# Attention on one core: every unit's finished row maxima go through DRAM with their parts made on VectorE, prepared weights are stored a task later, reciprocals come a key tile later

## The chip, the cores and the metric

The kernel runs on one core of one Trainium2 chip. The metric is device time in microseconds; a kernel's time is the median of its runs. A profiled execution is one further run, taken by the hardware profiler; its span reaches from its first to its last instruction.

The core's engines have one instruction queue each: TensorE (PE, matmuls into PSUM, with its weight loads as PEld), VectorE (DVE), ScalarE (ACT), GpSimd (POOL) and SyncE (SP), which issues nearly all of this kernel's DMAs.

## The reference

One transformer block for 2048 rows of width 640: attention with 32 heads of 20 columns, then a gated feed-forward layer of width 1728.

```python
def _A_ref(x, wqkv, wo):
    qkv = (x @ wqkv).reshape(B, S, 3, H, Dh)  # then split into q, k, v per head
    scores = jnp.einsum("bhqd,bhkd->bhqk", q, k) * (Dh ** -0.5)
    p = _softmax(scores, axis=-1)
    o = jnp.einsum("bhqk,bhkd->bhqd", p, v)
    return o.transpose(0, 2, 1, 3).reshape(B, S, D) @ wo

def _B_ref(x, w_gate, w_up, w_down):
    return (_silu(x @ w_gate) * (x @ w_up)) @ w_down

h = x + _A_ref(_layernorm(x, axis=-1), A_wqkv, A_wo)
h2 = h + _B_ref(_layernorm(h, axis=-1), B_w_gate, B_w_up, B_w_down)
```

The output is h2. All is float32. The softmax subtracts each row's maximum before the exponential.

## The kernel before, in words

The program has three stages: the projections to q, k and v (to about 317 us), the attention (to about 1437 us), and the output projection with the feed-forward layer.

**Units and key tiles.** The attention stage is a loop over 32 units u. A unit is one group g of 4 heads (u // 4) and one chunk of 512 queries (u % 4). Inside, a loop goes over 16 key tiles kt of 128 keys. A key tile of a unit is a string of steps, ORDER (L41), which alternates between "WsSmmSsM" and "WSsMMsSm". "s" and "S" are the scores of one head (L1303, a TensorE matmul, then an exponential on ScalarE, L1309); "W" is the weighing of the key tile two back (L1313, eight matmuls of the probabilities with the values), followed by what is due at this key tile; "m" and "M" are one step each of the maxima.

**The maxima** of later units are built ahead, three steps in each key tile (`max_one`): one matmul of queries with 512 keys into one of three PSUM banks `ps_max` (L274), and a VectorE reduction of that bank (L280). The list `rest` says which unit's step is next, and with it where a unit v is complete: v = 4g at key tile 5 of unit 4g − 1, v = 4g + 1 at key tile 15 of that unit, v = 4g + 2 at key tile 5 of unit 4g + 1, and v = 4g + 3 at key tile 10 of unit 4g + 2, the unit just ahead of it. The first, v = 1, is complete at key tile 10 of unit 0.

**What happens to complete maxima.** At the end of the key tile `max_all` (L287) reduces the unit's partial maxima and negates them: 128 query rows by 16 numbers (4 heads, 4 query tiles). They are needed as rows along the queries, in two float32r parts each (a rounded part and the rest), under the queries in `q_stk`: the scores' matmul of 62 rows takes the subtraction along, so a unit's first scores wait for them. Before, there are two ways to it.

- Nine units (v = 1, and every v = 4g + 3) go through `max_finish`, two key tiles later: a TensorE transpose (L319), a ScalarE copy as first part (L89), a VectorE subtraction as second part (L90), and four DMAs from SBUF to SBUF (L326).
- The other 22 go through DRAM. `max_parts` makes the two parts at once, on POOL (cast L295, subtract L296); `max_turn`, four key tiles later, transposes blocks of 32 by 32 on VectorE (L303) and stores them to `m_d` (L304); `max_load`, six key tiles after completion, loads the rows by four DMAs (L314). `m_d` has two places, for odd and even units.

Unit 0's own maxima go through `max_finish` inside the projection stage.

**The end of a unit.** A unit's sums of exponentials come out of the accumulator by a copy and four small DMAs (L1326). At key tile 4 of the next unit VectorE takes the reciprocals (L1334), SP stores them (L1336) and loads them spread over the partitions, as `rb` (L1342). At key tile 9 POOL multiplies the output by `rb` (L1348); at key tile 11 SP issues four stores of it to `o_d` (L1351). The last two units use key tiles 3, 6 and 7.

**Weights prepared on the side.** From unit 1 on, at every key tile but 3 and 4, one task of a list is taken at step W (`prepare_weights`): a load of raw weights (L1141, L1195), two empty tasks, sums on POOL (L1153 to L1158, L1211 to L1217), and pieces, each a cast and a subtraction on POOL (L1121, L1122). Each task first issues, on SP, the DMA stores of the pieces that stand in the list `stores` (L1112); a piece's store is thus issued with the task after it. SP's queue also takes the loads of queries, keys and values (L176, L193).

**SP's order.** SP issues its DMAs in program order. An instruction that must wait, for a piece that POOL hasn't finished, or for an earlier DMA, holds up all behind it.

Of the kernel before, what the change touches and what calls it, by code (L numbers as in the profile page):

```python
# [26 lines left out]
NC = S // CH  # L27
# [17 lines left out]
def tile_block(ctx: ExitStack, tc: tile.TileContext, x, wqkv, wo, wg, wu, wd, out):  # L45
    nc = tc.nc
# [41 lines left out]
    def split(src, hi, lo, lo_engine=nc.vector):  # L88
        nc.scalar.activation(hi, src, AF.Copy)  # L89
        lo_engine.tensor_tensor(out=lo, in0=src, in1=hi.bitcast(F32), op=ALU.subtract)  # L90
# [193 lines left out]
    def max_all(u):  # L284

        ends[u] = stk.tile([P, G * TPC], F32, name="neg", tag="neg", bufs=2)
        nc.vector.tensor_reduce(  # L287
            ends[u], mxs[u].rearrange("p b h t k -> p (b h t) k"), axis=AX.X, op=ALU.max, negate=True
        )

    def max_parts(u):

        neg = ends[u]
        both = ends[u] = stk.tile([P, 2, G * TPC], F32R, name="neg2", bufs=2)
        nc.gpsimd.tensor_copy(both[:, 0], neg)  # L295
        nc.gpsimd.tensor_tensor(  # L296
            out=both[:, 1], in0=neg, in1=both[:, 0].bitcast(F32), op=ALU.subtract
        )

    def max_turn(u):  # L300

        turned = stk.tile([P, 2 * G * TPC], F32, name="turned", bufs=2)
        nc.vector.transpose(turned, ends.pop(u).bitcast(F32).rearrange("p i n -> p (i n)"))  # L303
        nc.sync.dma_start(m_d[u % 2], turned)  # L304

    def max_load(u):

        n = 2 * TPC
        rows = m_d[u % 2].rearrange("(q i r) c -> i r q c", q=4, i=2)
        for b in range(2):  # L310
            for i in range(2):
                row = b * ROW + NPART + i
                dst = queries[u][row : row + 1].bitcast(F32).rearrange("r j c -> r (j c)")
                nc.sync.dma_start(dst, rows[i, b * n : (b + 1) * n])  # L314

    def max_finish(u):

        m = (ps_one if u else ps_max)()[: G * TPC, :P]
        nc.tensor.transpose(m, ends.pop(u), ident)  # L319
        parts = stk.tile([G * TPC, 2, P], F32R, name="m2", tag="m2", bufs=1)  # L320
        split(m, parts[:, 0], parts[:, 1], nc.vector)
        for b in range(2):
            for i in range(2):
                row = b * ROW + NPART + i
                first = b * 2 * TPC
                nc.sync.dma_start(  # L326
                    queries[u][row : row + 1].bitcast(F32).rearrange(
                        "r j (t p) -> r (j t) p", t=TPC
                    ),
                    parts[first : first + 2 * TPC, i, :].bitcast(F32),  # L330
                )
# [33 lines left out]
    with tc.tile_pool(name="pa", bufs=2) as pa:  # L365
# [244 lines left out]
        stores = []  # L610

        def store(*last, queue=nc.gpsimd):

            while stores:
                queue.dma_start(*stores.pop(0))
            stores.extend(last)
# [487 lines left out]
    def prepare_weights():  # L1104


        stores, count = [], [0]

        def store():
            while stores:  # L1110
                dst, t = stores.pop(0)
                nc.sync.dma_start(dst.bitcast(F32), t.bitcast(F32))  # L1112

# [123 lines left out]
        tasks = []  # L1237
        for f in range(NF):
            tasks += block(f)
        for f in range(0, NF, 2):  # L1240
            if f < NF - 2:
                tasks += rows((f, f + 1), True)
            if f in d_d:
                tasks += rows((f, f + 1), False)
        return tasks + [store]

    class Ring:

# [49 lines left out]
    def scores(u, kt, j, probs):  # L1298

        p, b = divmod(j, 2)  # L1300
        rows = slice(b * ROW, b * ROW + NPART + 2)
        ps = ps_one()
        nc.tensor.matmul(  # L1303
            ps,
            keys[u // NC][rows, p, kt * P : (kt + 1) * P],
            queries[u][rows, p, :],
            start=True, stop=True,
        )
        nc.scalar.activation(probs[p][:, b, :], ps, AF.Exp, scale=scale)  # L1309
# [45 lines left out]
    todo, tail, accs, later, full, now = [], [], {}, {}, [], [0]  # L1355
    singles = [[(*a, b) for a in rest] for b in range(2)]
    left = {u: sum(2 for a in rest if a[0] == u) for u in range(1, NU)}

    def next_max(b):
        if singles[b]:  # L1360
            a = singles[b].pop(0)
            max_one(*a)
            left[a[0]] -= 1
            if left[a[0]] == 0:
                full.append(a[0])

    def weigh_next():
        u, kt, probs = todo.pop(0)
        if kt == 0:
            accs[u] = psum.tile([P, CH], F32, name="acc", tag=f"ps_{last % 3}")  # L1370
        weigh(u, kt, probs, accs[u])
        if kt == NT - 1:
            queues = [nc.sync] if u + 1 < NU else [nc.scalar, nc.sync]
            tail.append((u, *row_sums(accs.pop(u), *queues)))
# [3 lines left out]
    for u in range(NU):  # L1378
        g, c = divmod(u, NC)
        if g == NG - 1 and c >= 2:  # L1380
            _, first, ln, flips, _ = ahead
            extra = [*first, *ln, lambda: None, *flips]
        for kt in range(NT):
            now[0] = u * NT + kt
            probs = [pp.tile([P, 2, CH], F32, name="probs") for _ in range(2)]
            heads = [[0, 2], [1, 3]]
            order = ORDER[now[0] % 2] if singles[0] or singles[1] else "WsSsS"
            for op in order:
                if op in "mM":
                    next_max(int(op == "M"))  # L1390
                elif op in "sS":
                    scores(u, kt, heads[op == "S"].pop(0), probs)
                else:
                    if len(todo) == 2:
                        weigh_next()
                    for f in later.pop(now[0], ()):
                        f()
                    if extra:
                        extra.pop(0)()
                    if preparing and u and kt not in (3, 4):  # L1400
                        preparing.pop(0)()
                    if now[0] == (NU - NC) * NT + 8:
                        unit_ring, last_ring = weight_rings()
                        unit_ring.fill()
                        last_ring.fill()
            todo.append((u, kt, probs))
            for v in full:
                max_all(v)
                if v % NC == NC - 1 or v == 1:
                    later.setdefault(now[0] + 2, []).append(lambda v=v: max_finish(v))  # L1410
                else:
                    max_parts(v)
                    later.setdefault(now[0] + 4, []).append(lambda v=v: max_turn(v))
                    later.setdefault(now[0] + 6, []).append(lambda v=v: max_load(v))
            full.clear()
            if kt == 6 and u + 3 < NU:
                load_queries(u + 3)
            if kt == 10 and u == 0:
                fill_ones(k_stk[1])
            if kt >= 8 and kt % 2 == 0 and c == 1 and g + 1 < NG:  # L1420
                load_keys(g + 1, slice((kt - 8) // 2 * CH, (kt - 6) // 2 * CH))
            if kt >= 8 and kt % 2 == 0 and c == 2 and g + 1 < NG:
                load_values(g + 1, (kt - 8) // 2 * TPC, (kt - 6) // 2 * TPC)

            sooner = u >= NU - 2
            if kt == (3 if sooner else 4) and tail:
                reciprocals(u - 1, tail[0][2], nc.sync)
                rb = spread(u - 1, nc.sync)
            if kt == (6 if sooner else 9) and tail:
                store_o(u - 1, tail[0][1], rb, nc.gpsimd, None)  # L1430
            if kt == (7 if sooner else 11) and tail:
                store_o(u - 1, tail.pop()[1], rb, None, nc.sync)
            if g == NG - 1 and c >= 1:
                at = 8 if sooner else NT - 4
                if kt == at:
                    ahead = projection(
                        c - 1, ps_max if c < NC - 1 else (lambda: ps_b())
                    )
                if kt in (at, at + 1, 12 if sooner else 14):
                    ahead[0][min(kt - at, 2)]()  # L1440
                    if kt == at + 1 and c < NC - 1:
                        ahead[4]()
            k = 2 * (u - NU + 8)
            if kt in (12, 13) and 0 <= k + kt - 12 < ND:
                if k + kt == 12:
                    assert not preparing
                    wo_hi = pc.tile([P, ND, D], F32R, name="wo_hi", bufs=1)
                    wo_lo = pc.tile([P, ND, D], F32R, name="wo_lo", bufs=1)
                load_wo(k + kt - 12)
            if kt in (2, 3) and 0 <= k + kt - 4 < ND:  # L1450
                split_wo(k + kt - 4)
# [573 lines left out]
```

## Time and profile before

| what | us |
|---|---|
| median of 3 runs | 2018.49 |
| lowest and highest run | 2018.06, 2019.48 |
| the profiled execution | 2017.19 |
| its span | 2015.4 |

The granted TensorE clock of the profiled execution is 1.00. In rows of the profile, a group of instructions is given as line, engine, operation, output<-inputs, sizes and count, then busy time and mean duration of one in ns, then the idle time of the engine just ahead of them, with what ended most of it. A row of a timeline begins with the start and the duration in us; what stands in brackets at its end is the idle time ahead of it and who ended it. Rows of SP ("SPq") are the issues of DMAs, not their transfers. The rows that the argument needs are shown where it uses them.

### The profile page before, as it was taken

How to read it: one execution, taken by the hardware profiler on the slowest of the kernel's cores; microseconds unless marked ns; L12 is line 12 of the kernel's file. 1: busy time of each engine (PE TensorE's matmuls, PEld its weight loads, DVE VectorE, ACT ScalarE, POOL GpSimd, SP SyncE). 2: the span in 40 equal slices, each digit the busy share in tenths (PEclk: the TensorE clock that was granted, in tenths of full speed). 3: DMA queues.
4: the chain of work that ended last, by engine and by line, in shares of the span. 5: the costliest groups of instructions: out<-in, count | busy, mean ns of one | idle time of the engine just before them, and what ended most of it. 6: DMA issues, size and time to landing. Idle time of an engine off the chain costs nothing.

```text
span 2015.4 us, 40030 instructions
## 1 busy us (share of the span) xinstructions
PE 2002.7 (99%) x14354; PEld 1247.8 (62%) x14354; DVE 1603.9 (80%) x2806; ACT 1437.1 (71%) x2819; POOL 796.8 (40%) x1190
## 2 busy tenths in 40 slices
PE   9999999999999999999999999999999999999999
PEld 8999995333333333333333333345598888888888
DVE  5677778888888888888888988886387666676677
ACT  4678878999999999999999999986633222212221
POOL 7465423333443443343400011011156444754555
PEclk9999999999999999999999999999999999999999
DMA  7777563352634544535513022321159654974642
GB/s 252 255 251 264 179 204 86 117 150 92 190 104 135 159 128 133 160 122 164 172 40 88 22 75 71 94 63 56 40 185 312 223 187 154 354 274 156 206 150 94
DMA packets 199340, 310.35 MB, mean 154 GB/s; under 512 B 53744, under 2 KB 87856, under 8 KB 198120
## 3 DMA queue, kind: packets, MB, share of 16 engines
q1 hardware_dynamic: 192552, 284.21, 43.8%
q0 software_dynamic: 6496, 23.60, 3.9%
q8 instruction: 114, 1.87, 0.4%
q14 instruction: 82, 0.67, 0.1%
q10 hardware_dynamic: 96, 0.00, 0.0%
HBM read 208.11 MB, written 99.19 MB: 152 GB/s over the span
## 4 chain that ended last, share of the span: by engine, by line
PE 96%; DMA 1%; DVE 1%; POOL 1%; issue 0%; ACT 0%; SPq 0%; POOLq 0%; DVEq 0%; ACTq 0%
PE acc L1313 24%; PE ps_a L1481 17%; PE ps_one L1303 15%; PE ps_max L274 12%; PE ps_one L643 10%; PE ps_b L1576 9%; PE ps_max L239 3%; PE ps_max L1031 2%; PE ps_b L1031 2%; PE ps_two L805 0%; PE ps_two L696 0%; DVE mx L261 0%; DMA rb<-r_d 0%; DVE mx L280 0%; PE ps_max L1066 0%
## 5 line engine op out<-in xcount | busy, mean ns | idle before, releaser
L1309 ACT ACTIVATE probs<-ps_one 128x512 f32<-128x512 f32 x2048 | 1056.1, 612 | 61.9 <-PE ps_one L1303 35.0
L280 DVE TENSOR_REDUCE mx<-ps_max 128x1 f32<-128x512 f32 x1472 | 924.5, 683 | 107.0 <-PE ps_one L1303 73.2
L1303 PE MATMUL ps_one<-q_stk,k_stk 62*128 62x512 f32 x2048 | 580.6, 449 | 1.0 <-DMA q_stk<-m_d 1.0
L1313 PE MATMUL acc<-probs,v_stk 128*32 128x512 f32 x4096 | 546.3, 605 | 0.1
L1303 PEld LDWEIGHTS ps_one<-q_stk,k_stk 62*128 62x128 f32 x2048 | 248.0, 184 | 436.6 <-ACT probs L1309 413.9
L274 PE MATMUL ps_max<-k_stk,q_stk 60*128 60x512 f32 x1472 | 374.9, 426 | 1.1 <-DVE mx L261 0.9
L274 PEld LDWEIGHTS ps_max<-k_stk,q_stk 60*128 60x128 f32 x1472 | 272.5, 186 | 29.7 <-DVE mx L280 2.8
L1698 DVE TENSOR_TENSOR tmp<-ps_a,tmp 128x512 f32<-128x512 f32 x208 | 141.2, 689 | 121.0 <-PE ps_a L1481 94.0
L261 DVE TENSOR_REDUCE mx<-ps_max 128x2 f32<-128x512 f32 x288 | 180.6, 684 | 63.8 <-PE ps_max L239 60.2
L1313 PEld LDWEIGHTS acc<-probs,v_stk 128*32 128x32 f32 x4096 | 80.9, 108 | 179.8 <-issue 167.9
L251 ACT ACTIVATE ps_max<-ps_max 128x512 f32<-128x512 f32 x288 | 151.6, 583 | 42.8 <-PE ps_max L239 40.2
L1576 PE MATMUL ps_b<-halves,yp 128*128 128x320 f32 x1032 | 178.7, 308 | 0.2 <-DVE h L1581 0.2
L1576 PEld LDWEIGHTS ps_b<-halves,yp 128*128 128x128 f32 x1032 | 165.2, 188 | 16.0 <-DVE h L1581 0.5
L1481 PE MATMUL ps_a<-t,units 128*128 128x512 f32 x624 | 162.5, 396 | 0.0
L90 POOL TENSOR_TENSOR yp<-y,yp 128x256 fp32r<-128x256 f32 x96 | 60.4, 630 | 186.9 <-ACT yp L89 186.9
L1481 PE MATMUL ps_a<-z,units 128*128 128x512 f32 x516 | 133.9, 394 | 0.0
L1481 PEld LDWEIGHTS ps_a<-t,units 128*128 128x128 f32 x624 | 112.6, 188 | 18.5
L1348 POOL TENSOR_TENSOR o<-o,rb 128x512 f32<-128x512 f32 x31 | 39.9, 1286 | 199.8 <-DMA q_stk<-m_d 72.7
L1581 DVE TENSOR_TENSOR h<-ps_b,h 128x320 f32<-128x320 f32 x248 | 109.7, 480 | 5.8 <-PE ps_b L1576 4.3
L643 PE MATMUL ps_one<-z_hi,w_lo 64*128 64x512 f32 x380 | 113.3, 392 | 0.0
L643 PE MATMUL ps_one<-z_lo,w_hi 64*128 64x512 f32 x380 | 112.1, 392 | 0.0
L643 PE MATMUL ps_one<-z_hi,w_hi 64*128 64x512 f32 x380 | 111.5, 393 | 0.0
(224 smaller groups left out, 2651.7 us busy)
## 6 DMA issues: line engine op xcount, KB each, us to landing
units<-w_d SPq DMA_DIRECT2D x186, 256.0 KB
w_d<-stage SPq DMA_DIRECT2D x106, 256.0 KB
halves<-j_d SPq DMA_DIRECT2D x70, 320.0 KB
j_d<-stage SPq DMA_DIRECT2D x42, 320.0 KB
k_stk<-k_d SPq DMA_DIRECT2D x64, 160.0 KB
q_stk<-q_d SPq DMA_DIRECT2D x64, 160.0 KB
raw<-k_d SPq DMA_DIRECT2D x62, 160.0 KB
raw<-q_d SPq DMA_DIRECT2D x54, 160.0 KB
```

Source lines behind the costliest of these rows:

```text
L251: nc.scalar.activation(ps, ps, AF.Relu)
L261: nc.vector.tensor_reduce(mx[:, b, :, t, kc], ps.rearrange("p (j n) -> p j n", j=2), axis=AX.X, op=ALU.max,)
L274: nc.tensor.matmul(ps, queries[u][rows, pair, t * P : (t + 1) * P], keys[u // NC][rows, pair, kc * CH : (kc + 1) * CH], start=True, stop=True,
L280: nc.vector.tensor_reduce(mxs[u][:, b, pair, t, kc : kc + 1], ps, axis=AX.X, op=ALU.max)
L643: nc.tensor.matmul(ps, a[rows], b[rows], start=(i == n == 0), stop=(i == 1 and n == last), skip_group_check=True,)
L1303: nc.tensor.matmul(ps, keys[u // NC][rows, p, kt * P : (kt + 1) * P], queries[u][rows, p, :], start=True, stop=True,)
L1309: nc.scalar.activation(probs[p][:, b, :], ps, AF.Exp, scale=scale)
L1313: nc.tensor.matmul(acc[32 * j : 32 * j + 32, :], values[u // NC][:, kt, j * VW : j * VW + 32], probs[j // 2][:, j % 2, :], start=(kt == 0) ...
L1481: nc.tensor.matmul(ps.rearrange("p (t n) -> p t n", t=TPC), w[k][:, i], z[k][:, :, j], start=(first and m == 0), stop=(last and m == len(n ...
L1576: nc.tensor.matmul(ps, a, b, start=(n == 0), stop=(n == len(pairs) - 1))
L1581: nc.vector.tensor_tensor(out=h, in0=ps, in1=h, op=ALU.add)
L1698: add = lambda out, ps, x: nc.vector.tensor_tensor(out=out, in0=ps, in1=x, op=ALU.add)
```

## The change

`max_parts` puts its cast and its subtraction on VectorE in the place of POOL. All 31 units from v = 1 on take the way through DRAM; the turn comes one key tile after completion (four before), the load three key tiles after (six before, and two for the way through TensorE). `max_finish` remains for unit 0 alone. In `prepare_weights` the list of stores keeps its newest piece for one task more, so each store is issued two tasks after its piece; the last task stores all. The reciprocals, their store and their spread load move from key tile 4 to 5, POOL's multiply from 9 to 10; the stores of the output stay at 11. In the last two units these stay as they were.

```diff
@@ max_parts
-        nc.gpsimd.tensor_copy(both[:, 0], neg)
-        nc.gpsimd.tensor_tensor(
+        nc.vector.tensor_copy(both[:, 0], neg)
+        nc.vector.tensor_tensor(
             out=both[:, 1], in0=neg, in1=both[:, 0].bitcast(F32), op=ALU.subtract
         )
@@ prepare_weights
-        def store():
-            while stores:
+        def store(left=1):
+            while len(stores) > left:
                 dst, t = stores.pop(0)
                 nc.sync.dma_start(dst.bitcast(F32), t.bitcast(F32))
...
-        return tasks + [store]
+        return tasks + [lambda: store(0)]
@@ the loop over key tiles
             for v in full:
                 max_all(v)
-                if v % NC == NC - 1 or v == 1:
-                    later.setdefault(now[0] + 2, []).append(lambda v=v: max_finish(v))
-                else:
-                    max_parts(v)
-                    later.setdefault(now[0] + 4, []).append(lambda v=v: max_turn(v))
-                    later.setdefault(now[0] + 6, []).append(lambda v=v: max_load(v))
+                max_parts(v)
+                later.setdefault(now[0] + 1, []).append(lambda v=v: max_turn(v))
+                later.setdefault(now[0] + 3, []).append(lambda v=v: max_load(v))
...
-            if kt == (3 if sooner else 4) and tail:
+            if kt == (3 if sooner else 5) and tail:
                 reciprocals(u - 1, tail[0][2], nc.sync)
                 rb = spread(u - 1, nc.sync)
-            if kt == (6 if sooner else 9) and tail:
+            if kt == (6 if sooner else 10) and tail:
                 store_o(u - 1, tail[0][1], rb, nc.gpsimd, None)
```

What this moves can be seen in the order of the instructions. First VectorE's queue in unit 3, around key tile 5, where the maxima of unit 4 (`mx_130`) are complete and those of unit 5 (`mx_131`) go on. Before:

```order
L280 TENSOR_REDUCE mx_131<-ps_max 128x1 x2
L287 TENSOR_REDUCE neg<-mx_130 128x16
L280 TENSOR_REDUCE mx_131<-ps_max 128x1 x9
L303 STREAM_TRANSPOSE turned<-neg_7288 128x32
L280 TENSOR_REDUCE mx_131<-ps_max 128x1 x21
```

After:

```order
L280 TENSOR_REDUCE mx_131<-ps_max 128x1 x2
L287 TENSOR_REDUCE neg<-mx_130 128x16
L295 CAST neg_7285<-neg 128x16
L296 TENSOR_TENSOR neg_7285<-neg,neg_7285 128x16
L1334 RECIPROCAL r<-r 128x16
L303 STREAM_TRANSPOSE turned<-neg_7285 128x32
L280 TENSOR_REDUCE mx_131<-ps_max 128x1 x30
```

Three reductions are one key tile. L287 and the transpose stood in two places, three key tiles apart; now five small operations stand between two reductions.

Then SP's queue in unit 14, behind the spread load `rb` and the loads of queries: `j_d` and `d_d` are prepared pieces that are stored, `raw` is a load of weights, `v_stk` one of values, `o_d` the output of unit 13, and `q_stk` takes the maxima of unit 15. Before:

```order
L1112 DMA j_d_96<-stage 128x640
L1195 DMA raw<-in_B_w_down 128x640 x2
L193 DMA v_stk_126<-v_d 128x4x96 x2
L1112 DMA d_d_90<-stage 128x640
L1351 DMA o_d<-o 20x512 x4
L326 DMA q_stk<-m_13092 1x8x128 x4
L1112 DMA d_d_90<-stage 128x640
L193 DMA v_stk_126<-v_d 128x4x96
```

After:

```order
L1112 DMA j_d_96<-stage 128x640
L1195 DMA raw<-in_B_w_down 128x640 x2
L193 DMA v_stk_126<-v_d 128x4x96 x2
L304 DMA m_d_71<-turned 128x32
L1112 DMA j_d_96<-stage 128x640
L1351 DMA o_d<-o 20x512 x4
L1112 DMA d_d_90<-stage 128x640
L193 DMA v_stk_126<-v_d 128x4x96
L314 DMA q_stk<-m_d_71 1x32x32 x4
```

The loads of the maxima have moved behind one more piece and one load of values, and a store of the maxima stands ahead of the output's stores.

Last POOL's queue at the same place, with the multiply of unit 13's output in it. Before:

```order
L1121 CAST stage<-sums 128x320
L1122 TENSOR_TENSOR stage<-sums,stage 128x320
L1348 TENSOR_TENSOR o<-o,rb 128x512
L1121 CAST stage<-raw 128x320
L1122 TENSOR_TENSOR stage<-raw,stage 128x320
```

After:

```order
L1121 CAST stage<-sums 128x320
L1122 TENSOR_TENSOR stage<-sums,stage 128x320
L1121 CAST stage<-raw 128x320
L1122 TENSOR_TENSOR stage<-raw,stage 128x320
L1348 TENSOR_TENSOR o<-o,rb 128x512
```

The multiply stands behind one piece more.

## The prediction

> **What bounds the kernel now.** I read the page first: the span, and the busy share of each engine.
>
> ```profile
> span 2015.4 us, 40030 instructions
> PE 2002.7 (99%) x14354; PEld 1247.8 (62%) x14354; DVE 1603.9 (80%) x2806; ACT 1437.1 (71%) x2819; POOL 796.8 (40%) x1190
> ```
>
> TensorE is busy for 99% of the span, so time is lost or won only where TensorE stands still, or where an instruction of its own comes or goes. The profiled execution took 2017.19 us, 1.8 us more than its span, and lies 1.3 us under the median of the three runs, 2018.49; I make the sum on 2017.2 and put 1.3 on at the end. A difference under 0.2%, about 4 us, is what a measurement of this kernel could not tell from no change.
>
> The change touches the attention stage, so next I read the busy times of 50 us inside it (columns: TensorE, weight loads, VectorE, ScalarE, POOL, granted clock, DMA share, GB/s), then VectorE's timeline in a quiet place.
>
> ```profile
> 850.00:900.00 50.00, 50.00 (x355) 19.48 (x349) 44.98 (x76) 48.82 (x96) 25.15 (x37) 1.00 0.43 150
> 926.12 1.89 DVE L280 TENSOR_REDUCE mx<-ps_max 128x1 f32<-128x512 f32 x3 [0.23 <-PE ps_one L1303]
> 928.23 1.29 DVE L280 TENSOR_REDUCE mx<-ps_max 128x1 f32<-128x512 f32 x2 [0.23 <-PE ps_one L1303]
> ```
>
> TensorE fills all 50 us at a granted clock of 1.00. A key tile lasts 928.23 − 926.12 = 2.11 us. In it VectorE reduces three banks of maxima without a pause (1.89 us) and then waits 0.23 us for TensorE. Those 0.23 us are all the room VectorE has, since its three banks of PSUM are what TensorE fills next: a VectorE that is late by more holds TensorE up. So the bound is TensorE, with VectorE close behind it.
>
> How much lateness reaches TensorE can be read off two places where the trace of before has VectorE late, because a reciprocal had to wait for its sums. For each, VectorE's rows come first, then TensorE's weighing matmuls, which stand once in each key tile. Unit 10:
>
> ```profile
> 670.72 1.89 DVE L280 TENSOR_REDUCE mx<-ps_max 128x1 f32<-128x512 f32 x3 [0.23 <-PE ps_one L1303]
> 673.75 0.25 DVE L1334 RECIPROCAL r<-r 128x16 f32<-128x16 f32 x1 [1.15 <-DMA r<-o]
> 673.92 1.82 DVE L280 TENSOR_REDUCE mx<-ps_max 128x1 f32<-128x512 f32 x3
> ```
>
> ```profile
> 673.19 1.06 PE L1313 MATMUL acc<-probs,v_stk 128*32 128x512 f32 x8
> ```
>
> and a key tile on
>
> ```profile
> 676.22 1.06 PE L1313 MATMUL acc<-probs,v_stk 128*32 128x512 f32 x8
> ```
>
> The next three reductions were due at 670.72 + 2.11 = 672.83 and came at 673.92, 1.09 late; TensorE took 3.03 us instead of 2.11, a loss of 0.92. Unit 18:
>
> ```profile
> 946.43 1.89 DVE L280 TENSOR_REDUCE mx<-ps_max 128x1 f32<-128x512 f32 x3 [0.23 <-PE ps_one L1303]
> ...
> 949.21 1.22 DVE L280 TENSOR_REDUCE mx<-ps_max 128x1 f32<-128x512 f32 x2
> ```
>
> ```profile
> 948.91 1.06 PE L1313 MATMUL acc<-probs,v_stk 128*32 128x512 f32 x8
> ```
>
> and a key tile on
>
> ```profile
> 951.50 1.07 PE L1313 MATMUL acc<-probs,v_stk 128*32 128x512 f32 x8
> ```
>
> They came at 949.21 instead of 948.54, 0.67 late; TensorE took 2.59, a loss of 0.48. So about 0.18 us of lateness is swallowed, and the rest is lost one for one.
>
> **The change part by part.** *The parts on VectorE.* Grouped by line over the attention stage (317 to 1437 us), these are the operations concerned.
>
> ```profile
> L1334 DVE RECIPROCAL r<-r 128x16 f32<-128x16 f32 x31 | 7.5, 243 | 1.9 <-DMA r<-o 1.9
> L287 DVE TENSOR_REDUCE neg<-mx 128x16 f32<-128x64 f32 x31 | 6.6, 214 | 0.6
> L303 DVE STREAM_TRANSPOSE turned<-neg 128x32 f32<-128x32 f32 x22 | 4.4, 200 | 0.0
> ```
>
> And the two on POOL that move:
>
> ```profile
> L296 POOL TENSOR_TENSOR neg<-neg,neg 128x16 fp32r<-128x16 f32 x22 | 4.9, 222 | 1.8
> L295 POOL CAST neg<-neg 128x16 fp32r<-128x16 f32 x22 | 4.3, 197 | 255.4 <-DVE neg L287 255.4
> ```
>
> Before, L287 (0.214) and the transpose (0.200) of a unit stood in two different gaps between threes of reductions, and each fits into 0.23 us. After, the order puts L287, cast, subtract, for 15 of the units the reciprocal too, and the transpose into one gap, since the transpose is now due one key tile later and at the head of it. VectorE's price for a cast and a subtract of 16 elements is not in this trace. The nearest rows are three small operations that depend on each other:
>
> ```profile
> 1503.18 0.17 DVE L99 TENSOR_TENSOR t_late<-t_late,v_late 128x8 f32<-128x8 f32 x1
> 1503.38 0.17 DVE L99 SCALAR_TENSOR_TENSOR r_late<-t_late,r_late 128x8 f32<-128x8 f32 x1
> ```
>
> A dependent operation starts 0.20 us after the one before it; an independent one starts before the other ends (the reciprocal at 673.75 lasts 0.25 and the reduction follows at 673.92, an overlap of 0.08). I take 0.20 each. Without the reciprocal the chain is L287 0.21 + cast 0.20 + subtract 0.20 + transpose 0.20 = 0.81, less an overlap of 0.08 at its end: 0.73 to 0.81. With the reciprocal it is about as long: the reciprocal depends on none of its neighbours, so it overlaps on both sides and adds about 0.08, and L287 there stands two reductions behind the last one that it needs, so it starts 0.08 early. I take 0.77 for both. Less the gap of 0.23 VectorE is 0.54 late, less 0.18 TensorE loses 0.36. Thirty units pay (v = 1 to 30; that of unit 31 falls where VectorE has nothing left to reduce): 30 × 0.36 = **+10.8**. Bounds: 0.17 a unit, 5 in all, if cast and subtract overlap so far that each adds 0.10; 0.5 a unit, 15 in all, if they cost 0.25 each.
>
> [...]
>
> [...] In one place of this trace a tiny VectorE operation beside a long POOL one was stretched to the other's end:
>
> ```profile
> 115.69 1.84 POOL L90 TENSOR_TENSOR z_lo<-z_lo 128x768 fp32r<-128x768 f32 x1 [2.05 <-ACT z_lo L89]
> 115.73 1.83 DVE L99 TENSOR_SCALAR r_a<-v_a 128x4 int32<-128x4 int32 x1
> ```
>
> POOL was busy 25.15 of the 50 us above, with prepared weights, and 20 of the 30 new pairs fall where it prepares them. If one of the two operations met half of a POOL operation of some 0.9 us each time it would be 20 × 0.5 × 0.45 = 4.5; if never, nothing. No small VectorE operation of the attention stage is stretched on average in the rows above, so I take **+2**, with 0 to 6.
>
> [...]
>
> *The transposes through TensorE.* Nine units lose their finish by a TensorE transpose, a ScalarE copy and a VectorE subtract. One of them:
>
> ```profile
> 343.54 1.06 PE L1313 MATMUL acc<-probs,v_stk 128*32 128x512 f32 x8
> 344.53 0.28 PE L319 MATMUL ps_one<-ident,neg 128*16 128x128 f32 x1
> ...
> 345.92 1.06 PE L1313 MATMUL acc<-probs,v_stk 128*32 128x512 f32 x8
> ```
>
> That key tile took 2.38 instead of 2.11: 0.27 × 9 = **−2.4**. ScalarE's nine copies go too, and it does not set the pace.
>
> *Old stalls that go.* The two reciprocals that waited (0.92 and 0.48) come a key tile later, 2.1 us, more than the 1.15 they waited. And unit 18's first scores waited for their maxima, whose load now starts three key tiles earlier, at key tile 8 instead of 11:
>
> ```profile
> 932.86 3.21 SPq L314 DMA_DIRECT2D q_stk<-m_d  x4
> ```
>
> ```profile
> 937.44 0.47 PE L1303 MATMUL ps_one<-q_stk,k_stk 62*128 62x512 f32 x1 [1.01 <-DMA q_stk<-m_d]
> ```
>
> 0.92 + 0.48 + 1.0 = **−2.4**. These rows also give the tail of such a load: issuing ends at 936.07, and TensorE goes on 1.4 us later.
>
> *What is queued on SP.* SP issues in order, and each row below is an issue. The unit looked at is 14, where the maxima of unit 15 are completed at key tile 10. SP's queue first, then POOL, then TensorE's first scores of unit 15.
>
> ```profile
> 812.74 0.59 SPq L1342 DMA_DIRECT2D rb<-r_d  x1
> ```
>
> ```profile
> 819.20 1.08 SPq L1195 DMA_DIRECT2D raw<-in_B_w_down  x2
> ```
>
> ```profile
> 827.46 1.55 SPq L1351 DMA_DIRECT2D o_d<-o  x4
> 829.11 2.82 SPq L326 DMA_DIRECT2D q_stk<-m  x4
> 832.03 0.39 SPq L1112 DMA_DIRECT2D d_d<-stage  x1
> 832.48 0.43 SPq L193 DMA_DIRECT2D v_stk<-v_d  x1
> ```
>
> ```profile
> 819.49 1.28 POOL L1348 TENSOR_TENSOR o<-o,rb 128x512 f32<-128x512 f32 x1 [14.17 <-DMA rb<-r_d]
> 825.64 0.45 POOL L1121 CAST stage<-raw 128x320 fp32r<-128x320 f32 x1 [4.87 <-DMA raw<-in_B_w_down]
> 826.18 0.88 POOL L1122 TENSOR_TENSOR stage<-raw,stage 128x320 fp32r<-128x320 f32 x1
> ```
>
> ```profile
> 833.64 0.51 PE L1303 MATMUL ps_one<-q_stk,k_stk 62*128 62x512 f32 x2
> ```
>
> Issue of rb at 812.74 to its landing, which frees SP for the raw load, was 6.5 us, and the raw load fed POOL 6.4 us after its issue. Here the maxima were ready 1.4 us after 831.93, at 833.3, 0.3 us ahead of the scores that need them. With the reciprocal a key tile later, rb and the raw load come up to 2.1 us later, and POOL's multiply now stands behind the first piece: it starts at 827.0 at the earliest, at 829.1 if the raw load is 2.1 later, and ends between 828.3 and 830.4. Behind it SP issues the stores of o (1.55), now also one prepared piece (0.39) and one load of values (0.43), and only then the four loads of maxima (2.82): issued by 833.5 to 835.6, usable 834.9 to 837.0 against 833.64. TensorE would stand 1.3 to 3.3 us in the place of 0.3 us of slack; I take 1.8, nearer the lower end, because only the first of the four must land for the first scores. The same order stands in units 6, 10 and 18; I take 1.8 for units 10, 14 and 18 and nothing for 6, where there is more slack: **+5**, with 0 to 10.
>
> *At nothing:* POOL losing its casts and 255.4 us in line for VectorE (it is not on the path; if it were late, rb's multiply would be, which is the SP term); the stores a task later, which fill a queue that waits for POOL anyway and would cost one 0.39 us issue if not. *Sum:* 2017.2 + 10.8 + 2 + 5 − 2.4 − 2.4 = 2030.2, and 1.3 to the median: **2031.5 us**.
>
> **The rivals.** *Faster: the chain is hidden.* If cast and subtract run back to back with their neighbours, the gap grows to under 0.41 us and TensorE swallows it, the queue is no later than before, and only the gains are left: 2018.5 − 4.8 = 2013.7. For it: 0.23 + 0.18 us are free, and the old waits are real. Against: L287 and the transpose alone fill 0.41. Chance 0.10. *No change.* The chain at its low end, +5, against the gains of 4.8, and all loads in time: 2018.7. Chance 0.13. *Slower, but SP in time.* 10.8 + 2 − 4.8: 2026.5. It decides whether the four loads land before TensorE comes to the next unit; for it, TensorE itself comes later by what VectorE costs. Chance 0.30. *The forecast*, VectorE and SP both late, 2031.5 and up to 2044 with each term at its upper end: 0.47.
>
> **How the numbers follow.** Slower is the last two, 0.77; same 0.13; faster 0.10. Leaving out the faster case and the upper end of the forecast leaves out about 2 in 10: from 2018.5 (chain at 5, no lateness on SP) to 2040.
>
> **What would show it.** In the profile after: gaps of about 0.77 us between threes of reductions at each unit's completion, with the next weighing 0.36 us late, 30 times; nothing left of a TensorE wait on the transposes; casts and subtracts of L295 and L296 at about 0.2 us, longer beside POOL; and TensorE's first scores of units 11, 15 and 19 waiting for q_stk from m_d by some 1.8 us each. The prediction is wrong if weighing stays at 2.11 us apart across these gaps, or if the waits on m_d are nought.

## The result and the profile after

The changed kernel takes 2038.51 us (median of 5 runs, 2035.59 to 2042.63); the kernel before, measured again with it, 2018.49 (2016.96 to 2020.14). The ratio is 1.0101, with a 95% interval of 1.009 to 1.0112: the change makes the kernel 20 us slower. The profiled execution took 2040.52 us, against 2017.19 for that of before: 23.3 us to be explained in the two traces.

The page's span and busy times of the changed kernel:

```profile
span 2038.7 us, 40000 instructions
PE 2019.2 (99%) x14345; PEld 1251.8 (61%) x14345; DVE 1612.5 (79%) x2868; ACT 1437.9 (71%) x2810; POOL 786.0 (39%) x1146
```

TensorE has nine instructions fewer and is busy 16.5 us longer. VectorE gained only 8.6 us of work. So most of the lost time counts as busy on TensorE, though its work did not grow, and the busy share doesn't tell where a span went. The two traces are therefore compared key tile by key tile, by the distance from one key tile's first exponential (L1309) to the next one's. These exponentials start between 318.3 and 1452.9 us in the trace of before, so the stage ends some 16 us later than the 1437 us given above, and between 320.2 and 1475.1 in the trace of after. Places that differ by more than 0.1 us, in sums (us):

```text
30 key tiles behind the chain on VectorE, where no operation in it was stretched   0.36 to 0.47 each: +12.3
the same places, what stretched operations add                                     +3.2
8 places that had a transpose through TensorE                                       -0.26 each: -2.1
units 10 and 18: reciprocals and first scores that waited before                    -0.92 -0.48 -1.13 = -2.5
starts of units 7, 11, 15, 19                                                       0.78 + 3.15 + 2.83 + 0.44 = +7.2
unit 0, key tiles 1 and 2                                                           +2.9
before the attention stage +1.9, after it +1.1                                      +3.0
```

The sum is 24.0 against 23.3; the small differences that the table leaves out come to −0.7. The last line need not be the change's: over the 13 traces of this study the stage's first exponential starts anywhere from 318.3 to 323.0 us, though no edit touches what is ahead of it, and the trace of before is the earliest. Now the views that carry these lines. First the chain itself: VectorE in unit 3, at the place whose order was shown above.

```profile
441.30 0.21 DVE L287 TENSOR_REDUCE neg<-mx 128x16 f32<-128x64 f32 x1
441.54 0.17 DVE L295 CAST neg<-neg 128x16 fp32r<-128x16 f32 x1
441.75 0.17 DVE L296 TENSOR_TENSOR neg<-neg,neg 128x16 fp32r<-128x16 f32 x1
441.92 0.25 DVE L1334 RECIPROCAL r<-r 128x16 f32<-128x16 f32 x1
442.09 0.15 DVE L303 STREAM_TRANSPOSE turned<-neg 128x32 f32<-128x32 f32 x1
442.17 3.63 DVE L280 TENSOR_REDUCE mx<-ps_max 128x1 f32<-128x512 f32 x6
```

From L287's start to the next reduction are 0.87 us. TensorE's weighing matmuls around it:

```profile
441.96 1.06 PE L1313 MATMUL acc<-probs,v_stk 128*32 128x512 f32 x8
444.49 1.06 PE L1313 MATMUL acc<-probs,v_stk 128*32 128x512 f32 x8
```

They start 2.53 us apart; the one ahead of them (439.84) stands 2.12 before the first. Six reductions then run without a pause, as they did behind the late reciprocals of before. So much for the chain alone. At the start of unit 8 VectorE and POOL stand like this:

```profile
602.07 0.22 DVE L287 TENSOR_REDUCE neg<-mx 128x16 f32<-128x64 f32 x1
602.32 0.68 DVE L295 CAST neg<-neg 128x16 fp32r<-128x16 f32 x1
603.04 0.66 DVE L296 TENSOR_TENSOR neg<-neg,neg 128x16 fp32r<-128x16 f32 x1
```

```profile
601.55 0.73 POOL L1154 TENSOR_TENSOR sums<-sums,raw 128x256 f32<-128x256 f32 x1
602.24 0.73 POOL L1157 TENSOR_TENSOR sums<-raw 128x256 f32<-128x256 f32 x1
602.94 0.73 POOL L1158 TENSOR_TENSOR sums<-raw,sums 128x256 f32<-128x256 f32 x1
```

Cast and subtract take 0.68 and 0.66 instead of 0.17 each; both end about where a POOL operation does (602.97, 603.67). That key tile lost 1.38 us, not 0.38. The means of the groups are 229 and 215 ns, against 175 in most of the 31 places, where nothing disturbs them: (54 + 40) ns × 31 = 2.9 us, near the 3.2 of the key tiles. Five casts and four subtracts carry it (0.30 us and more each).

```profile
L295 DVE CAST neg<-neg 128x16 fp32r<-128x16 f32 x31 | 7.1, 229 | 1.1
L296 DVE TENSOR_TENSOR neg<-neg,neg 128x16 fp32r<-128x16 f32 x31 | 6.7, 215 | 1.1
L287 DVE TENSOR_REDUCE neg<-mx 128x16 f32<-128x64 f32 x31 | 6.7, 215 | 0.6
```

L287, a reduction, kept its time: 0.215 us on average, 0.214 before.

Then TensorE's waits, in the list of waits (total, times, longest):

```profile
PE ps_one L1303 <- DMA q_stk<-m_d: 3.5, 4, 1.5
...
PE ps_one L1303 <- ACT probs L1309: 1.4, 2, 0.8
```

The kernel before had one such wait on `m_d`, 1.0 us. How the longest came about can be followed in unit 14, on SP, on POOL and on TensorE:

```profile
832.18 3.60 SPq L1195 DMA_DIRECT2D raw<-in_B_w_down  x2
...
844.29 1.41 SPq L1351 DMA_DIRECT2D o_d<-o  x4
845.75 0.34 SPq L1112 DMA_DIRECT2D d_d<-stage  x1
846.13 0.43 SPq L193 DMA_DIRECT2D v_stk<-v_d  x1
846.61 2.78 SPq L314 DMA_DIRECT2D q_stk<-m_d  x4
```

```profile
841.62 0.45 POOL L1121 CAST stage<-raw 128x320 fp32r<-128x320 f32 x1 [15.23 <-DMA raw<-in_B_w_down]
842.15 0.87 POOL L1122 TENSOR_TENSOR stage<-raw,stage 128x320 fp32r<-128x320 f32 x1
842.98 1.29 POOL L1348 TENSOR_TENSOR o<-o,rb 128x512 f32<-128x512 f32 x1
```

```profile
849.47 0.47 PE L1303 MATMUL ps_one<-q_stk,k_stk 62*128 62x512 f32 x1 [1.47 <-DMA q_stk<-m_d]
851.05 0.47 PE L1303 MATMUL ps_one<-q_stk,k_stk 62*128 62x512 f32 x1 [1.11 <-DMA q_stk<-m_d]
```

The raw weights arrive at 841.6, POOL makes one piece of them before it may multiply, the output's stores wait for the multiply until 844.29, and the loads of the maxima stand behind those, with two other issues between. TensorE gets them 1.47 and 1.11 us late, first for one pair of heads, then for the other.

Last, what was not in the forecast at all. At the start of unit 11 TensorE waits twice:

```profile
706.77 0.46 PE L1303 MATMUL ps_one<-q_stk,k_stk 62*128 62x512 f32 x1 [0.63 <-DMA q_stk<-m_d]
707.99 0.47 PE L1303 MATMUL ps_one<-q_stk,k_stk 62*128 62x512 f32 x1 [0.76 <-ACT probs L1309]
```

The second wait is put down to ScalarE, but it is the wait for the second half of the maxima that unit 15 shows with its own name: in the trace the last of the four loads lands at 707.85, and TensorE goes on at 707.99. Then the granted clock (the seventh entry, between POOL's busy time and the DMA share) falls:

```profile
705.00:709.00 4.00, 2.61 (x21) 1.00 (x23) 2.07 (x4) 2.65 (x7) 3.76 (x8) 1.00 0.56 169
709.00:713.00 4.00, 4.00 (x23) 1.41 (x21) 2.79 (x6) 3.47 (x8) 1.84 (x4) 0.57 0.60 187
713.00:717.00 4.00, 4.00 (x34) 1.67 (x30) 2.98 (x5) 3.14 (x7) 0.00 (x0) 1.00 0.59 194
```

In the trace's record of the clock it is 0.5 for 3.41 us from 709.32 on, 1.7 us lost behind 1.4 us of waiting; and 0.5 for 6.83 us from 323.62 on, in unit 0, 2.4 us behind the end of a wait of 0.93, which costs the 2.9 us of the table. The wait, and the busy times behind it:

```profile
321.25 0.50 PE L274 MATMUL ps_max<-k_stk,q_stk 60*128 60x512 f32 x1 [0.93 <-DVE mx L261]
```

```profile
325.00:331.00 6.00, 6.00 (x29) 2.18 (x22) 2.27 (x4) 2.29 (x5) 5.00 (x2) 0.55 0.39 129
```

That wait in unit 0 stands in the trace of before too, where the clock kept 1.00. So part of the 20 us is clock: the five runs were granted 0.997, 0.999, 0.996, 0.998 and 0.999, in the order of 2040.52, 2035.59, 2042.63, 2038.51 and 2037.78 us. Each 0.001 is 2.04 us of such a run; put back to a full clock, all five lie by that estimate between 2033.6 and 2035.7 (to about 1 us, since the clock is given to 0.001). The change costs some 16 us by work and waits, and its runs lose 2 to 8 by the clock. Runs of the kernel before can lose some too: of the nine measured beside the first experiments, one was granted 0.997 and took 2025.55 us, against a median of 2017.97.

### The profile page after: what moved, and what is told of

Its sections match the earlier page's. It is cut to its first block, busy times and chain, and to the rows that moved or that the text cites. A ratio compares the mean times of both kernels' runs of the same rounds, so it can differ in the third digit from the quotient of the medians.

```text
span 2038.7 us, 40000 instructions
## 1 busy us (share of the span) xinstructions
PE 2019.2 (99%) x14345; PEld 1251.8 (61%) x14345; DVE 1612.5 (79%) x2868; ACT 1437.9 (71%) x2810; POOL 786.0 (39%) x1146
## 4 chain that ended last, share of the span: by engine, by line
PE 92%; DMA 4%; DVE 2%; SPq 1%; POOL 1%; issue 0%; ACT 0%; DVEq 0%; POOLq 0%; ACTq 0%
PE acc L1313 23%; PE ps_a L1478 16%; PE ps_one L1303 15%; PE ps_max L274 12%; PE ps_one L643 10%; PE ps_b L1573 8%; PE ps_max L239 3%; PE ps_max L1031 2%; PE ps_b L1031 1%; DVE mx L280 1%; DMA v_stk<-v_d 1%; DMA rb<-r_d 1%; DMA raw<-q_d 1%; PE ps_two L805 0%; DMA o_t<-o_d 0%
## 5 line engine op out<-in xcount | busy, mean ns | idle before, releaser
L1309 ACT ACTIVATE probs<-ps_one 128x512 f32<-128x512 f32 x2048 | 1057.4, 610 | 80.9 <-PE ps_one L1303 55.0
L274 PE MATMUL ps_max<-k_stk,q_stk 60*128 60x512 f32 x1472 | 384.0, 427 | 2.1 <-DVE mx L261 0.9
L274 PEld LDWEIGHTS ps_max<-k_stk,q_stk 60*128 60x128 f32 x1472 | 268.1, 186 | 43.0 <-DVE mx L280 20.1
```

The source lines that it names most:

```text
L274: nc.tensor.matmul(ps, queries[u][rows, pair, t * P : (t + 1) * P], keys[u // NC][rows, pair, kc * CH : (kc + 1) * CH], start=True, stop=True,
```

## The experiments

Theory A is the prediction's: VectorE's chain in one gap, and loads of maxima that SP issues too late because of the later reciprocals. The rivals were that VectorE's chain costs nothing (B), that the later stores or the way through DRAM make the loads late (C, F), and that VectorE pays for any operation wherever it stands (D). All intervals are 95%, against the kernel before on the same chip (its medians 2017.97, 2016.8 and 2017.47 in the three sets).

### Reciprocals and multiply back

```diff
-            if kt == (3 if sooner else 5) and tail:
+            if kt == (3 if sooner else 4) and tail:
...
-            if kt == (6 if sooner else 10) and tail:
+            if kt == (6 if sooner else 9) and tail:
```

> The changed kernel with reciprocals back at key tile 4 and POOL's multiply back at 9. Theory A (the loads of maxima are late on SP because of the later reciprocals): the waits for q_stk from m_d go, -7; the reciprocal leaves VectorE's chain, 15 x 0.17 = -2.5; the two old waits of a reciprocal for its sums return, +1.4: about 2030. Theory C (the loads are late because of the stores that are kept a task longer, or because the load waits for its own store): the waits stay, about 2037.

Measured: 2028.95 us, ratio 1.0046 (1.0029 to 1.0062). TensorE has no wait on `m_d` left. The later reciprocals and multiply cost 9.6 us in this surrounding, where the expectation had 8.5. The two old waits of a reciprocal, which it had coming back, stay away; and the reciprocal in the chain was worth less than written, 0.05 to 0.12 us a unit where nothing was stretched (in unit 3 a loss of 0.40 became 0.32), not 0.17.

### Stores back

```diff
-        def store(left=1):
+        def store(left=0):
```

> The changed kernel with every prepared piece stored at the next task again. Theory A: the late loads remain, 2036 to 2040. Theory C: the waits for q_stk from m_d go, about 2031.

Measured: 2038.67 us, ratio 1.0095 (1.0079 to 1.0112), no different from the changed kernel. The waits on `m_d` stay (4.5 us in four). The later stores cost and bring nothing that shows.

### The maxima alone

The kernel with both of the edits above.

> Of the change only the part on the maxima: parts on VectorE, transpose a key tile later, load three later, for all units; reciprocals, multiply and stores as in the kernel before. Theory A: 2018.5 + 30 x 0.39 for the chain less 15 x 0.17 for the reciprocal that isn't in it, + 3 beside POOL, - 1.7 for the transposes through TensorE, - 1.1 for unit 18's load: about 2028. Theory B: 2016 to 2019.

Measured: 2029.18 us, ratio 1.0057 (1.0041 to 1.0073). B falls. TensorE's waits on `m_d` are nearly gone, and the time is still up by 11 us:

```profile
PE ps_one L1303 <- DMA q_stk<-m_d: 0.2, 1, 0.2
```

Its granted clock was 1.00 through the attention stage, and its lost key tiles are the chain's: 0.29 to 0.34 more than before at the places from which the reciprocal has gone, 0.38 to 0.43 at the others, more beside POOL.

### The cast made twice

```diff
         nc.vector.tensor_copy(both[:, 0], neg)
+        nc.vector.tensor_copy(both[:, 0], neg)
```

in the kernel with the maxima alone.

> The maxima's part of the change alone (as e4_maxima_alone, 2029.2), with the cast on VectorE made twice. Theory A: one operation more in the chain is lost one for one, 30 x 0.2 = 6, and some 1 us more beside POOL: about 2036. Rival (other waits hide it, or the chain isn't what TensorE waits for): 2029.

Measured: 2036.25 us, ratio 1.0094 (1.0081 to 1.0108), 7.1 us more. Compared key tile by key tile with the maxima alone, 25 of the 30 places lost 0.17 to 0.25 us more, the other five 0.31 to 0.88, in units whose POOL is at work. At the undisturbed places one operation more in the chain cost about its start-to-start time, 0.21 us in the chain at 1252 us of its trace (1252.36 to 1252.57), one for one.

### Reciprocals and multiply alone, in the kernel before

```diff
-            if kt == (3 if sooner else 4) and tail:
+            if kt == (3 if sooner else 5) and tail:
...
-            if kt == (6 if sooner else 9) and tail:
+            if kt == (6 if sooner else 10) and tail:
```

> Of the change only the reciprocals, multiply a key tile later, in the kernel before. Theory A (late rb and multiply push the loads of the maxima of v = 4g + 3 past the unit's start, by whichever way they go): the loads from SBUF stand right behind the output's stores, some 0.8 us earlier than in the changed kernel, so the waits of units 11 and 15 are about 1 to 2 each and the total +4, about 2022, with q_stk<-m as the releaser. Theory E (the later reciprocals hurt only together with the way through DRAM): 2017 to 2019.

Measured: 2024.13 us, ratio 1.0037 (1.0025 to 1.005): some 7 us, more than written. E falls, since it hurts by itself. In its trace 1.7 of the 7 us are the clock's (0.5 for 3.41 us from 666.12 on, behind two late loads). The list of waits shows both ways late, the loads from SBUF (`m`) and those through DRAM, which in this kernel are due at key tile 11:

```profile
PE ps_one L1303 <- DMA q_stk<-m_d: 3.5, 4, 0.9
```

```profile
PE ps_one L1303 <- DMA q_stk<-m: 1.3, 2, 0.9
```

That the loads of v = 4g + 2 (units 10 and 18 here) would be late too was not foreseen.

### Only the multiply back, only the reciprocals back

Each is one half of the first experiment's diff.

> The changed kernel with POOL's multiply alone back at key tile 9, the reciprocals still at 5. Theory G (the loads of maxima are late because the multiply stands behind the first prepared piece, and the output's stores behind the multiply): most of the 7 us go, what is left is a prepared piece's store that stands ahead of the loads, about 1 us in unit 15: 2032 to 2034. Theory H (the late rb, and with it the late raw load, is the cause by itself): 2038.

> The changed kernel with the reciprocals alone back at key tile 4, the multiply still at 10. Theory G and H each for a part: the raw load is back in time, so the piece and the multiply end some 2 us earlier than in the changed kernel and the loads are late by 1 us or so in units 11 and 15; the reciprocal leaves VectorE's chain, -1.5: 2031 to 2034. If the multiply's place alone decided: 2037. If the reciprocals' place alone decided: 2029, as with both back.

Measured: 2032.29 us with the multiply back (ratio 1.007, 1.0056 to 1.0084), 2031.55 with the reciprocals back (1.0066, 1.0053 to 1.0078). Both were expected about there. Starts of units lost 0.86 + 0.27 + 0.32 us in the one (7, 11, 15) and 0.75 + 0.48 in the other (11, 15), against 7.2 in the changed kernel. So neither edit alone is the cause of the long waits: they take both the late raw weights and the multiply behind their first piece.

### The transpose a key tile later

```diff
-                later.setdefault(now[0] + 1, []).append(lambda v=v: max_turn(v))
+                later.setdefault(now[0] + 2, []).append(lambda v=v: max_turn(v))
```

> Everything as in the changed kernel, but the transpose and its store come two key tiles after completion instead of one, so the transpose has a gap of its own. Theory A (the chain of small VectorE operations in one gap costs about 0.4 us a unit, 12 in all): where no reciprocal stands in the chain the transpose adds 0.2 us to it, where one does it adds 0.08; so 15 x 0.2 + 15 x 0.08 = 4 us less, about 2034.5. Theory B (VectorE's chain costs nothing, the 20 us are late loads of maxima and what follows from them): 2038.5, or more, since the store before the load is issued a key tile later.

Measured: 2041.33 us, ratio 1.0115 (1.0096 to 1.0133), a miss of 7 us. The chain did what it should: at its undisturbed places 0.19 to 0.25 us less without the reciprocal and some 0.10 with it. But the store of the maxima now stands behind the output's stores, the load waits for it, and TensorE and its clock pay. The clock of unit 15's first 7 us, after a wait of 2.58:

```profile
849.71 0.76 PE L1303 MATMUL ps_one<-q_stk,k_stk 62*128 62x512 f32 x1 [2.58 <-DMA q_stk<-m_d]
```

```profile
849.00:856.00 7.00, 5.83 (x22) 2.69 (x22) 2.16 (x4) 3.57 (x7) 1.75 (x3) 0.51 0.66 217
```

The waits on `m_d` sum to 8.3 us in eight, and the clock fell behind three of the unit starts (7, 11, 15; 0.60 and 0.55 in the two 4 us from 705 us on, at unit 11). The expectation had said "or more" for theory B alone; it holds for A as well.

### The parts on VectorE, spread over two key tiles

The kernel with the maxima alone, and in it, with a list `soon` that is looked at behind each reduction of a key tile:

```diff
-                max_parts(v)
-                later.setdefault(now[0] + 1, []).append(lambda v=v: max_turn(v))
+                soon.setdefault((now[0] + 1, 1), []).append(lambda v=v: max_parts(v))
+                at = (now[0] + 1, 2) if v % NC == NC - 1 else (now[0] + 2, 1)
+                soon.setdefault(at, []).append(lambda v=v: max_turn(v))
```

> The maxima's part of the change alone, with the same operations on VectorE, but not in one gap: L287 in its gap, cast and subtract behind the first reduction of the next key tile, the transpose behind the first reduction of the key tile after that (for v = 4g + 3 behind the second reduction of the same key tile, so that its load is not late). Theory A (only what doesn't fit in VectorE's 0.23 us of idle time a key tile and the 0.18 that are swallowed is lost): the 11 us of the chain go, but for 8 x 0.2; the gains stay (-1.7, -2.5); beside POOL some +1.5: about 2017.5. Theory D (each operation that VectorE gets costs its duration wherever it stands, 30 x 0.4): 2026 to 2029, as with the maxima alone.

Measured: 2031.77 us, ratio 1.0076 (1.0062 to 1.009): a miss by 14. The operations did not become free. Behind a chain 0.11 to 0.24 us were lost where nothing was stretched, 5 us in all, half of before the spreading. As the timelines read, cast and subtract between two reductions delay the other two of the same three by 0.4, and the 0.23 us of idle time come only behind them. And POOL still stretches some of the operations, by more than before. In unit 18:

```profile
969.03 0.69 DVE L280 TENSOR_REDUCE mx<-ps_max 128x1 f32<-128x512 f32 x1
969.64 0.85 DVE L295 CAST neg<-neg 128x16 fp32r<-128x16 f32 x1
970.53 1.20 DVE L296 TENSOR_TENSOR neg<-neg,neg 128x16 fp32r<-128x16 f32 x1
971.65 0.68 DVE L280 TENSOR_REDUCE mx<-ps_max 128x1 f32<-128x512 f32 x1
```

Cast and subtract take 2.0 us in the place of 0.37, and TensorE lost 1.92 in that key tile. Besides, reciprocals waited 6.1 us for their sums (1.9 in the kernel before); why the small DMAs of the sums are later here was not followed up. The median is also 3 us above the profiled execution that these numbers are from. The time settles nothing between A and D, since it is above both; at the undisturbed places the loss is neither A's next to nothing nor D's 0.4 us.

### The parts on POOL, all units through DRAM

The kernel with the maxima alone and the list `soon` of the last one, with the parts on POOL and made at completion, as in the kernel before. Against the maxima alone:

```diff
-        nc.vector.tensor_copy(both[:, 0], neg)
-        nc.vector.tensor_tensor(
+        nc.gpsimd.tensor_copy(both[:, 0], neg)
+        nc.gpsimd.tensor_tensor(
...
-                later.setdefault(now[0] + 1, []).append(lambda v=v: max_turn(v))
+                soon.setdefault((now[0] + 1, 1), []).append(lambda v=v: max_turn(v))
```

> All 31 units through DRAM with the load three key tiles after completion, as in the changed kernel, but with the parts on POOL and the transpose behind the first reduction of the next key tile; reciprocals, multiply and stores as before. Theory A: VectorE's extra is L287 and a transpose in two places, which fit; the gains of -1.7 and -2.5 are left, and up to 0.6 of a late load: about 2015. Theory F (the way through DRAM itself, its store and loads on SP, costs time): 2018 or more.

Measured: 2034.11 us, ratio 1.0085 (1.0071 to 1.0099): a miss by 19, in three places. Behind 26 of the 30 completions no key tile is longer than in the kernel before by 0.1 us, and behind one it is by 0.34: the chain is gone. In units 10, 14 and 18 a key tile lost 5.92, 4.12 and 5.35. VectorE there:

```profile
686.56 0.22 DVE L287 TENSOR_REDUCE neg<-mx 128x16 f32<-128x64 f32 x1
686.75 0.69 DVE L280 TENSOR_REDUCE mx<-ps_max 128x1 f32<-128x512 f32 x1
691.89 0.21 DVE L303 STREAM_TRANSPOSE turned<-neg 128x32 f32<-128x32 f32 x1 [4.45 <-POOL neg L296]
```

POOL had two sums, the multiply and two more sums ahead of the cast, which it began at 691.36. VectorE stood 4.45 us behind a transpose that nobody needed yet, and TensorE 3.88 behind VectorE; the clock's record has 0.5 there for 6.83 us from 691.24 on. Theory F isn't what made this kernel slow: no wait on `m_d` stands in TensorE's list. What it shows is the price, 4.45 us of VectorE here, of an engine that waits in order for another.

### The load sooner, in the kernel before

```diff
-                    later.setdefault(now[0] + 4, []).append(lambda v=v: max_turn(v))
-                    later.setdefault(now[0] + 6, []).append(lambda v=v: max_load(v))
+                    later.setdefault(now[0] + 2, []).append(lambda v=v: max_turn(v))
+                    later.setdefault(now[0] + 4, []).append(lambda v=v: max_load(v))
```

> The kernel before with one edit: the 22 units that go through DRAM are transposed two key tiles after completion (four before) and loaded four after (six before); parts stay on POOL, nine units stay on TensorE's transpose. Theory A (the old waits of unit 10's and 18's reciprocals and of unit 18's first scores go because the load of maxima leaves SP's queue earlier): -2.5 at no price, about 0.13% under the kernel before. Rival (they went for the later reciprocals or for VectorE's own lateness): no difference.

Measured: 2017.6 us (11 runs) against 2017.47 (15), ratio 1.0004 (0.9995 to 1.0013): no difference, and the 2.5 us that the traces promise are outside the interval. In its trace the three old waits are gone (0.92, 1.14 and 0.47 us less in these key tiles), so earlier loads do remove them; but 1.4 us went to a halved clock in unit 0, behind the same wait of 0.92 as ever, and 0.8 to unit 8. Whether other runs of the kernel before have the old waits is not known, and it stays open where the gain of its other runs went.

## Why the prediction was right, and where it was off

The direction was right, and the median of 2038.51 lies in the range, near its upper end; the likeliest value, 2031.5, was 7 us short. Both mechanisms that it names, VectorE's chain and SP's late loads, are shown by the experiments; that the median stayed inside the range although the clock was left out is owed to a wide upper end. Step by step:

- **The bound** was read rightly: TensorE, with VectorE 0.23 us behind it. What carried over was the calibration: 0.18 us swallowed and the rest one for one, from two late reciprocals. Forecast 0.36 us a unit, measured 0.36 to 0.47; +10.8 forecast, +12.3 found. That the reciprocal adds 0.08 held (0.05 to 0.12). The doubled cast shows the one for one by itself.
- **The price of cast and subtract**, 0.20 from start to start, came out as 0.21 to 0.24 in the chain shown (441.30 to 441.54 to 441.75), with durations of 0.17.
- **Beside POOL** +2 was written and +3.2 found. The reason given for the lower value, that no small operation of the attention stage was stretched on average, was weak: L287 and the transpose aren't stretched in the new trace either, cast and subtract are, up to five times (0.88 us in unit 18).
- **The transposes through TensorE** brought 0.26 us at eight places, 2.1 in all, and not 2.4: the ninth, in unit 30, shows no gain.
- **The old waits** went, with about the size forecast (2.4 forecast, 2.5 found), but not for the reason given for the reciprocals. They also go with the reciprocals at key tile 4; in the last experiment the earlier load of the maxima alone removes them. That it does so by leaving SP's queue before the sums need it is read from the order of the queue, not tested.
- **SP's queue** was the step with the most working, and it held in kind: multiply behind the first piece, that behind the raw load, stores and loads behind the multiply. In unit 14 the loads were forecast 1.3 to 3.3 us late; they cost 2.8. The choice of 1.8, "because only the first of the four must land", failed there, since the second half's loads were late as well. Unit 7, for which nothing was set down, lost 0.8; unit 19 only 0.4. Waits came to 5.5 us in all, near the +5, but that is partly luck: three times 1.8 was written, and 1.4, 2.8 and 0.4 came, with 0.8 in a place that was not in the sum.
- **The term that was missing** is the clock. The trace of before has it at 1.00 through the attention stage, though TensorE waits up to 1.01 us there. The prediction counted a wait at its length. In the changed kernel's trace 1.7 us behind the waits of unit 11 and 2.9 in unit 0 are the clock's, and its median run lost some 4 us to it, by its granted 0.998. The clock (4.6 us in that trace) and 3.0 outside the attention stage are most of the 10.3 us by which the sum, 13.0, missed the 23.3; the rest is in the terms above. The 1.3 us put on for the median went the wrong way: the profiled execution of after lies 2.0 above its median.
- **Stores a task later**, costed at nothing: nothing, in both surroundings in which it was tried.

## What to carry to other kernels

Before work is moved to an engine that stands one step behind the bound, read its idle time per period there, not its busy share: a VectorE that is busy for 80% of the span looks as if it had room, and 0.23 us a key tile was all there was. Here L287 (0.21 us) and the transpose (0.20) fitted one by one into those 0.23; side by side with cast, subtract and reciprocal they took 0.87 in unit 3, the chains of the units cost TensorE 0.36 to 0.47 each, and spread over two key tiles still 0.11 to 0.24. The loads of unit 15's maxima, issued in order behind the output's stores, came 1.47 and 1.11 us late with them, so a step that is moved by one period should be followed through each queue that it passes.

## What was not expected of the hardware

Short waits of TensorE cost more here than their length. In the changed kernel's trace the clock of the attention stage fell to 0.5 twice: for 6.83 us from 323.62 on, behind the wait of 0.93 us in unit 0, and for 3.41 us from 709.32 on, behind 0.63 + 0.76 us in unit 11. It did not fall behind 1.47 + 1.11 us in unit 15 (1.00 from 849 to 856), and in the trace of before, where unit 0 has the same wait of 0.93 (it ends at 319.40), it did not fall either. In other kernels it fell within 2.58 us (unit 15 with the later transpose, 0.51 from 849 to 856) and 3.88 (parts on POOL). The gap's length alone does not decide.

What the two traces show besides, with no edit that tests it: both falls come a whole number of times 3.413 us, the length of the shorter one, behind the first full clock at 6.18 us, 317.44 us or 93 of them for unit 0's and 703.15 us or 206 for unit 11's. Cut from there into stretches of 3.413 us, TensorE was busy for 59% of the one ahead of unit 11's fall (705.91 to 709.32). The two gaps of unit 15 lie in two stretches (845.86 to 852.68, 63 and 62%), those of unit 11 in one. So it may matter how the gaps lie to the stretches. Unit 0 doesn't fit: 70% ahead of its fall (320.20 to 323.62) is more than unit 15's 63 and 62%, behind which none came, and in the trace of before 73% (316.12 to 319.54, with the wait of 0.93 in it) was followed by none. What decides is not shown.

VectorE's cast and subtract of 128x16 took 0.17 to 0.18 us at most places of the changed kernel's trace and up to 0.88 beside POOL's operations, with the parts spread over two key tiles up to 1.20. Of the 62 in the changed kernel's trace nine took 0.30 us and more, and each of the nine ended 0.03 to 0.04 us behind the end of an operation of POOL. L287, a reduction, kept its 215 ns on average, 208 to 222 in that trace.
